# Constant bounds for the experts' places, and counts taken at attention's end

## The chip, the cores and the metric

The kernel runs on one core of one Trainium2 chip. Its measure is the device time in microseconds (us) of one execution of the program. Three runs before the change took 791.21, 792.16 and 792.94 us; the median is 792.16 us. The inputs are drawn once, from a fixed seed.

## The reference, cut to what matters

The program is three layers behind one another, all in 32-bit floats. `x` has 1536 rows (2 batches of 768) and 512 columns.

```python
scores = scale * q @ k.T - slope * dist          # 8 heads, 64 wide
scores = where(first 8 columns or the last 96, scores, -1e9)
x = softmax(scores) @ v                          # attention

expert_idx = argmax(norm(x) @ norm(emb).T / tau) # 8 experts, one per row
for e in range(8):                               # first mixture
    mask = expert_idx == e
    out[mask] = gate_w[mask] * (relu(x[mask] @ w1[e]) @ w2[e])   # 512 -> 1024 -> 512

for e in range(4):                               # second mixture: every row through all four
    out2 += p[:, e] * (relu(out @ v1[e]) @ v2[e])
```

How many rows an expert gets is known only while the program runs. The reference's own routing of its drawn inputs gives the eight experts 171, 247, 155, 177, 135, 215, 231 and 205 rows.

## The kernel before

**Stages.** Attention runs first, over 12 tiles of 128 rows. At its end the rows are scattered to `xs`, a buffer in DRAM with 256 places (`CAP`) for each expert. Then the first mixture goes through the experts one by one, and the second mixture through four experts in two halves each, over chunks of 512 columns.

**The first mixture.** An expert has eight steps (`st`), each with one quarter of its weights: four steps of first products `h` (lines 907 to 909) and four of second products `y` (lines 922 and 923). A number is kept as a high and a low part (`wh`, `wl`; `xh`, `xl`; the two halves of `hhl`), so each weight block takes part in three products for `h`, and in one double-width and one single-width product for `y`. ScalarE writes the high parts, VectorE the low ones. A quarter is split six or seven steps before it is used.

**Arms by rows.** An expert's products need only as many columns as it has rows. Three widths exist, 184, 232 and 256, and TensorE branches on a register (`wide`) that `wider(e)` loads from the table `arm`. `h` has two arms (232, 256), `y` three, once for each of eight half-quarters `f`. Expert 0 has no arms: when its work begins, the counts are not there yet, so both its products run at 256.

**The counts.** In step 1 of expert 0, `offsets()` multiplies `cum` with ones on TensorE (line 793), and from it VectorE makes `cnt` (line 798), `over` and `arm`. GpSimd adds the counts up one by one (line 805) to `off`, the first place of each expert in the list of rows without gaps, and casts it to `offi` (line 806).

**Places.** After expert `e`'s products, a register `o_` is loaded from `offi` (line 943) with the bounds 0 and 1536, and the results go to 256 columns of `x2h` (ScalarE, line 775) and `x2l` (VectorE, line 948) from column `o_` on. What lies behind an expert's own rows is overwritten by the next expert, so the order of the experts is kept. The framework orders readers of `x2h` and `x2l` after all writers whose columns may overlap theirs, by the bounds of `o_`.

**The second mixture** begins with `Unit.hidden` (lines 1039 to 1041): twelve products of 512 columns for each of its blocks, from columns 0 to 511 of `x2h` and `x2l` first. The instructions are written in program order on each engine; the framework adds the waits.

Of the kernel before, what the change touches and what calls it, by code (L numbers as in the profile page):

```python
# [22 lines left out]
P = 128  # L23
# [13 lines left out]
def tile_attention_moe_moe(ctx: ExitStack, tc: tile.TileContext, q, k, v, n_global, n_local,  # L37
# [166 lines left out]
    base = cp.tile([P, T], F32, name="base")  # L204
    rsb = cp.tile([P, T, 8], F32, name="rsb")
    offi = cp.tile([P, NE], I32, name="offi")

    pc = ring.tile([P, 1024], F32, tag="w", name="pc")
    perm = pc[:, 0:2 * CAP].rearrange("p (i n) -> p i n", i=2)
# [82 lines left out]
    def count(t_, pp):  # L292

        while small and small[0][0] <= t_:
            fill()
        nc.tensor.matmul(pp, tri, oh[:, t_, :], start=True, stop=False)
        nc.tensor.matmul(pp, ones, cum[:, t_, :], start=False, stop=True)
        pps[t_] = pp
# [12 lines left out]
                                     xall[:, t_, :], None, bounds_check=NSLOT - 1, oob_is_err=False)  # L311

    xy = []

    def first_rows(xe):
        for i in range(2):
            for c in range(KD):
                nc.tensor.matmul(xy[c][:, i * P:(i + 1) * P], xe[:, i, c * P:(c + 1) * P], ident, start=False, stop=False)  # L320
# [6 lines left out]
    with ExitStack() as at:  # L327
# [387 lines left out]
        rows_x(T - 1, 1)  # L715
        xy.extend([ps_s.tile([P, CAP], F32, tag="s", name="xy") for _ in range(4)])
        add_rows(T - 2)
        count(T - 1, ps_a.tile([P, NE], F32, tag="at", name="pp"))
        fin2(T - 1)
        first_rows(xe)  # L720
        add_rows(T - 1)
        xh0, xl0 = (ring.tile([P, 1024], F32R, tag="w", name="x0").rearrange("p (k n) -> p k n", k=KD) for _ in range(2))
        for c in range(KD):
            nc.scalar.copy(xh0[:, c, :], xy[c])
# [41 lines left out]
    with ExitStack() as mo:  # L766
# [15 lines left out]
        with ExitStack() as m1:  # L782
# [6 lines left out]

            def offsets():  # L790

                pt = ps_t.tile([P, NE], F32, tag="t", name="t")
                nc.tensor.matmul(pt, ones, cum[:, T, :], start=True, stop=True)
                cnt = mp1.tile([P, NE + 1], F32, name="cnt")
                over = mp1.tile([P, NE], F32, name="over")
                arm = mp1.tile([P, NE], I32, name="arm")
                off = mp1.tile([P, NE], F32, name="off")
                nc.vector.tensor_tensor(cnt[:, 0:NE], pt, ebase, ALU.subtract)
                nc.vector.tensor_scalar(over, cnt[:, 0:NE], float(WIDTHS[0]), None, ALU.is_gt)
                nc.vector.scalar_tensor_tensor(arm, cnt[:, 0:NE], float(WIDTHS[1]), over, ALU.is_gt, ALU.add)  # L800
                nc.vector.tensor_reduce(cnt[:, NE:], cnt[:, 0:NE], AX.X, ALU.max)
                nc.vector.scalar_tensor_tensor(flag, cnt[:, NE:], float(CAP) + 0.5, fl[:, 0:1], ALU.is_ge, ALU.max)
                nc.gpsimd.memset(off[:, 0:1], 0.0)
                for e in range(1, NE):
                    nc.gpsimd.tensor_tensor(off[:, e:e + 1], off[:, e - 1:e], cnt[:, e - 1:e], ALU.add)
                nc.gpsimd.tensor_copy(offi, off)
                nc.gpsimd.tensor_tensor(off, off, ebase, ALU.subtract)
                return off, arm

            def offsets2(off):  # L810

# [8 lines left out]
            def records(ri):  # L820
# [2 lines left out]
                    nc.gpsimd.indirect_dma_start(recv[t_], bass.IndirectOffsetOnAxis(ap=ri[:, t_:t_ + 1].bitcast(U32), axis=0),  # L823
                                                 rsrc[:, t_, :], None, bounds_check=NT - 1, oob_is_err=False)
                nc.gpsimd.dma_start(out=rsb, in_=rec.rearrange("(t p) c -> p t c", p=P))

            def wider(e):
                return nc.values_load(sorted_[2][0:1, e:e + 1], engines=(mybir.EngineType.PE,), min_val=0, max_val=2)

            def two_widths(e, wide):  # L830

                if e == 0:
                    yield CAP
                else:
                    with tc.If(wide > 1) as full:
                        yield WIDTHS[2]
                    with full.Else():
                        yield WIDTHS[1]

            def three_widths(e, wide):  # L840

                if e == 0:
                    yield CAP
                else:
                    with tc.If(wide > 0) as over:
                        with tc.If(wide > 1) as full:
                            yield WIDTHS[2]
                        with full.Else():
                            yield WIDTHS[1]
                    with over.Else():  # L850
                        yield WIDTHS[0]

            xr = {}

# [23 lines left out]
            def side(st):  # L878

                if st == 1:  # L880
                    sorted_[0], sorted_[2] = offsets()
                if st == 2:
                    sorted_[1] = offsets2(sorted_[0])
                    nc.gpsimd.memset(x2l.bitcast(F32), 0.0)
                if 2 <= st < 2 + T:
                    square(mp1, st - 2)
                if st == 3 or 2 + T <= st:
                    next(parts, None)
                if st == 8 + T:
                    records(sorted_[1])  # L890
# [1 line left out]
            load_x(1)  # L892
            hp = cycle([ps_h.tile([P, 2, CAP], F32, tag="h", name="h") for _ in range(3)])
            yp = ps_y.tile([P, KD, 2, CAP], F32, name="y")
            wide = None
            for e in range(NE):
                xa, xb = (xh, xl) if e else (xh0, xl0)
                for i in range(4):
                    st = 8 * e + i
                    wh, wl = use(st)  # L900
                    pt = next(hp)
                    for w_ in two_widths(e, wide):
                        for f in range(2):
                            ws = slice(f * P, (f + 1) * P)
                            for c in range(KD):
                                o_, a_, b_ = pt[:, f, 0:w_], xa[:, c, 0:w_], xb[:, c, 0:w_]
                                nc.tensor.matmul(o_, wh[:, c, ws], a_, start=c == 0, stop=False)  # L907
                                nc.tensor.matmul(o_, wh[:, c, ws], b_, start=False, stop=False)  # L908
                                nc.tensor.matmul(o_, wl[:, c, ws], a_, start=False, stop=c == KD - 1)  # L909
                    relu3(pt, hhl[:, 2 * i:2 * i + 2, 0, :], hhl[:, 2 * i:2 * i + 2, 1, :])  # L910
                    split_to(min(st + PRE, W0 + 2))
                    side(st)
                for i in range(4):
                    st = 8 * e + 4 + i
                    wh, wl = use(st)
                    for f in range(2):
                        kf = 2 * i + f
                        for w_ in three_widths(e, wide):
                            a_ = hhl[:, kf, :, 0:w_]
                            for d in range(KD):  # L920
                                ws = slice(d * P, (d + 1) * P)
                                nc.tensor.matmul(yp[:, d, :, 0:w_], wh[:, f, ws], a_, start=kf == 0, stop=False, skip_group_check=True)  # L922
                                nc.tensor.matmul(yp[:, d, 0, 0:w_], wl[:, f, ws], a_[:, 0], start=False, stop=kf == KF - 1, skip_group_check=True)  # L923
# [8 lines left out]
                    if e == NE - 1:  # L932
# [5 lines left out]
                        elif i == 2:  # L938
# [2 lines left out]
                            w_op(0, 3)  # L941
                wide = ahead
                o_ = nc.values_load(offi[0:1, e:e + 1], engines=(mybir.EngineType.Activation, mybir.EngineType.DVE),
                                    min_val=0, max_val=NT)
                for d in range(0, KD, 2):
                    hi, lo = (a[:, d:d + 2, bass.ds(o_, CAP)] for a in (x2h, x2l))
                    split3(yp[:, d:d + 2, 0, :], hi, rest)
# [414 lines left out]
```

## Time and profile before

| | us |
|---|---|
| median of three runs | 792.16 |
| the profiled execution | 791.21 |
| its span, first to last instruction | 789.5 |
| attention's stage | 0 to about 96 |
| first mixture, expert 0 | 95.9 to 119.75 |
| first mixture, to the last `y` product | 119.75 to 269.85 |
| second mixture | 269.85 to the end |

TensorE is busy in 774.6 of the 789.5 us. A group of instructions in the profile has its line, engine, operation, what it writes and reads, its shape, its count, its busy time and mean duration, and the idle time before it. A matmul's duration reaches from its start to its modelled end, and the next one starts before that; how long a series takes is therefore read from the starts, or from a window that holds the series. [...]

### The profile page before, as it was taken

What the parts mean: (1) busy time and instruction counts of PE and PEld (TensorE: products, weight loads), DVE (VectorE), ACT (ScalarE), POOL (GpSimd) and SP (SyncE); (2) the same over time, 40 slices, a digit from 0 to 9 for tenths busy, and PEclk for the clock granted to TensorE, in tenths of its full rate; (3) what the DMA queues carried; (4) which work ended last, traced back from release to release, by engine and by line L of the source; (5) the groups of instructions that cost most, each with busy time, mean ns of one, the idle gap of its engine ahead of it and who ended that gap; (6) DMA issues with size and microseconds to landing.
All of it is one profiled execution on the core that took longest, in us unless ns stands there. A gap on an engine that the chain in (4) does not pass through costs nothing.

```text
span 789.5 us, 14345 instructions
## 1 busy us (share of the span) xinstructions
PE 774.6 (98%) x5450; PEld 706.5 (89%) x5450; DVE 547.1 (69%) x1306; ACT 354.0 (45%) x712; POOL 261.7 (33%) x240
## 2 busy tenths in 40 slices
PE   8999999999999899999999999999999999999996
PEld 5889899999999789999899999999899999989995
DVE  7888676877777446556766766766777766676674
ACT  7899576756655344442232242332233233224221
POOL 2026560160000621451361351352163145136222
PEclk9999999999999999999999999999999999999999
DMA  7996366677765400010000100010001001000111
GB/s 230 319 292 215 127 221 209 213 221 248 238 222 188 154 28 27 28 54 27 28 27 27 54 28 27 27 54 28 27 27 54 28 27 54 1 1 1 54 55 57
DMA packets 32313, 77.97 MB, mean 99 GB/s; under 512 B 3864, under 2 KB 10280, under 8 KB 32224
## 3 DMA queue, kind: packets, MB, share of 16 engines
q1 hardware_dynamic: 29792, 70.36, 27.2%
q0 software_dynamic: 2416, 6.39, 2.2%
q8 instruction: 58, 0.95, 0.5%
q14 instruction: 31, 0.25, 0.1%
q10 hardware_dynamic: 16, 0.02, 0.0%
HBM read 66.22 MB, written 10.53 MB: 97 GB/s over the span
## 4 chain that ended last, share of the span: by engine, by line
PE 84%; DVE 9%; ACT 3%; DMA 1%; issue 1%; POOL 1%; POOLq 0%; ACTq 0%; SPq 0%; DVEq 0%
PE h L1040 10%; PE h L1039 10%; PE h L1041 10%; PE z L1133 9%; PE z L1136 9%; PE z L1135 9%; PE y L922 7%; PE h L907 4%; PE h L909 4%; PE h L908 4%; PE y L923 3%; DVE sh L1090 2%; PE s L501 2%; PE o L542 1%; PE at L528 1%; ACT aa L520 1%
## 5 line engine op out<-in xcount | busy, mean ns | idle before, releaser
L1009 DVE SCALAR_TENSOR_TENSOR xall<-z,rsb,xall 128x256 f32<-128x256 f32 x313 | 135.2, 478 | 35.2 <-PE z L1136 34.6
L1040 PE MATMUL h<-x2l,wh 128*128 128x512 f32 (+1 forms) x400 | 153.5, 384 | 1.2 <-DVE x2l L948 1.2
L1039 PE MATMUL h<-x2h,wh 128*128 128x512 f32 (+1 forms) x400 | 153.5, 384 | 0.9 <-ACT x2h L775 0.9
L1041 PE MATMUL h<-x2h,wl 128*128 128x512 f32 (+1 forms) x400 | 152.7, 382 | 0.0
L1133 PE MATMUL z<-wt,sh 128*128 128x256 f32 x384 | 109.4, 285 | 0.8 <-ACT sh L1098 0.3
L1136 PE MATMUL z<-wt,sl 128*128 128x256 f32 x384 | 108.9, 284 | 0.0
L1135 PE MATMUL z<-wt,sh 128*128 128x256 f32 x384 | 108.6, 283 | 0.0
L1061 POOL TENSOR_TENSOR bl<-h,bh 128x512 fp32r<-128x512 f32 (+1 forms) x25 | 31.9, 1275 | 189.0 <-PE z L1136 164.5
L1076 ACT ACTIVATE ah<-h 128x512 fp32r<-128x512 f32 (+1 forms) x50 | 29.1, 582 | 140.6 <-PE h L1041 140.6
L1040 PEld LDWEIGHTS h<-x2l,wh 128*128 128x128 f32 x400 | 75.8, 189 | 14.9 <-POOL wt L182 1.3
L1039 PEld LDWEIGHTS h<-x2h,wh 128*128 128x128 f32 x400 | 75.7, 189 | 14.6 <-POOL t L175 1.2
L1041 PEld LDWEIGHTS h<-x2h,wl 128*128 128x128 f32 x400 | 75.5, 189 | 14.7
L922 PE MATMUL y<-hhl,wh 128*128 128x464 f32 (+2 forms) x256 | 82.6, 378 | 0.0
L1133 PEld LDWEIGHTS z<-wt,sh 128*128 128x128 f32 x384 | 73.5, 191 | 3.2 <-DVE xall L1009 1.8
L1049 ACT ACTIVATE h<-h 128x512 f32<-128x512 f32 (+1 forms) x50 | 28.7, 573 | 105.1 <-PE h L1041 105.1
L93 DVE TENSOR_TENSOR wl<-raw,wh 128x1024 fp32r<-128x1024 f32 x62 | 75.0, 1230 | 0.0
L1135 PEld LDWEIGHTS z<-wt,sh 128*128 128x128 f32 x384 | 73.6, 192 | 0.8
L1136 PEld LDWEIGHTS z<-wt,sl 128*128 128x128 f32 x384 | 73.5, 192 | 0.3 <-DVE sl L1099 0.3
L182 POOL TENSOR_TENSOR wt<-raw,wt 128x512 fp32r<-128x512 f32 x40 | 51.5, 1297 | 57.7 <-ACT wt L181 50.5
L123 ACT ACTIVATE wh<-raw 128x1024 fp32r<-128x1024 f32 x61 | 64.0, 1057 | 14.2 <-DMA raw<-in_moe_w_dram 12.6
L1055 DVE SCALAR_TENSOR_TENSOR ss<-h,h 128x256 f32<-128x256 f32 (+1 forms) x50 | 20.5, 409 | 69.6 <-ACT h L1049 69.6
L923 PE MATMUL y<-hhl,wl 128*128 128x232 f32 (+2 forms) x256 | 67.8, 265 | 0.0
(210 smaller groups left out, 1894.1 us busy)
## 6 DMA issues: line engine op xcount, KB each, us to landing
raw<-in_moe_w_dram SPq DMA_DIRECT2D x96, 512.0 KB, 3.9
xs<-zt SPq DMA_DIRECT2D x4, 1024.0 KB, 7.3
xr<-xs SPq DMA_DIRECT2D x14, 256.0 KB, 4.7
v<-in_v_dram SPq DMA_DIRECT2D x12, 256.0 KB, 5.4
k<-in_k_dram SPq DMA_DIRECT2D x11, 256.0 KB, 5.2
q<-in_q_dram SPq DMA_DIRECT2D x11, 256.0 KB, 5.0
vwin<-in_v_dram SPq DMA_DIRECT2D x10, 192.0 KB, 5.6
xe<-xs SPq DMA_DIRECT2D x2, 256.0 KB, 2.8
```

What stands on the lines that cost most here:

```text
L93: eng.tensor_tensor(lo, r, hi.bitcast(F32), ALU.subtract)
L123: nc.scalar.activation(hi, r, AF.Copy)
L182: nc.gpsimd.tensor_tensor(t[:, 1], src, t[:, 0].bitcast(F32), ALU.subtract)
L922: nc.tensor.matmul(yp[:, d, :, 0:w_], wh[:, f, ws], a_, start=kf == 0, stop=False, skip_group_check=True)
L923: nc.tensor.matmul(yp[:, d, 0, 0:w_], wl[:, f, ws], a_[:, 0], start=False, stop=kf == KF - 1, skip_group_check=True)
L1009: nc.vector.scalar_tensor_tensor(a_, src[:, i], w_, a_, ALU.mult, ALU.add)
L1039: nc.tensor.matmul(pt, wh[:, d, ws], x2h[:, d, cs], start=d == 0, stop=False)
L1040: nc.tensor.matmul(pt, wh[:, d, ws], x2l[:, d, cs], start=False, stop=False)
L1041: nc.tensor.matmul(pt, wl[:, d, ws], x2h[:, d, cs], start=False, stop=d == KD - 1)
L1133: nc.tensor.matmul(pt[:, i], hh[:, f, ts_], wh[:, f, :], start=(o_ < 3 or pt is not prods[o_][3]) and i == f == 0, stop=False, skip_group_ ...
L1135: nc.tensor.matmul(pt[:, i], hh[:, f, ts_], wl[:, f, :], start=False, stop=False, skip_group_check=True)
L1136: nc.tensor.matmul(pt[:, i], hl[:, f, ts_], wh[:, f, :], start=False, stop=f == 1, skip_group_check=True)
```

## The change

Two things are changed.

First, the counts are summed at attention's end. The tile `pp` of the last count gets a second half, which two small products fill with the sums of all rows; `sizes()` makes `cnt`, `over` and `arm` from it on VectorE, and the register for expert 0 is loaded there (`ahead = wider(0)`). So expert 0's `y` goes through three arms like the others'; its `h` stays at 256. Because a narrow arm leaves columns of `yp` unwritten, VectorE sets columns 184 to 255 to zero in step 1.

Second, the place `o_` of expert `e` gets the bounds max(0, 1536 - 256 (8 - e)) and min(1536, 256 e), which hold whenever no expert has over 256 rows. For expert 0 both are 0, so its place is a constant on VectorE. So that the table keeps within the bounds in every case, `offi` is now the larger of `off` and a table `least`, taken by VectorE, instead of a cast by GpSimd.

```diff
+    def sizes(pt):
+        nc.vector.tensor_tensor(cnt[:, 0:NE], pt, ebase, ALU.subtract)
+        nc.vector.tensor_scalar(over, cnt[:, 0:NE], float(WIDTHS[0]), None, ALU.is_gt)
+        nc.vector.scalar_tensor_tensor(arm, cnt[:, 0:NE], float(WIDTHS[1]), over, ALU.is_gt, ALU.add)
+    def wider(e):
+        return nc.values_load(arm[0:1, e:e + 1], engines=(mybir.EngineType.PE,), min_val=0, max_val=2)
...
-        count(T - 1, ps_a.tile([P, NE], F32, tag="at", name="pp"))
+        pp = ps_a.tile([P, 2, NE], F32, tag="at", name="pp")
+        count(T - 1, pp[:, 0])
+        nc.tensor.matmul(pp[:, 1], ones, cum[:, T - 1, :], start=True, stop=False)
+        nc.tensor.matmul(pp[:, 1], ones, oh[:, T - 1, :], start=False, stop=True)
         fin2(T - 1)
+        sizes(pp[:, 1])
         first_rows(xe)
         add_rows(T - 1)
+        ahead = wider(0)
...
-                pt = ps_t.tile([P, NE], F32, tag="t", name="t")
-                nc.tensor.matmul(pt, ones, cum[:, T, :], start=True, stop=True)
...
-                nc.vector.tensor_tensor(cnt[:, 0:NE], pt, ebase, ALU.subtract)
-                nc.vector.tensor_scalar(over, cnt[:, 0:NE], float(WIDTHS[0]), None, ALU.is_gt)
-                nc.vector.scalar_tensor_tensor(arm, cnt[:, 0:NE], float(WIDTHS[1]), over, ALU.is_gt, ALU.add)
...
-                nc.gpsimd.tensor_copy(offi, off)
+                least = mp1.tile([P, NE], I32, name="least")
+                nc.gpsimd.iota(least, [[CAP, NE]], base=NT - NE * CAP, channel_multiplier=0)
+                leastf = mp1.tile([P, NE], F32, name="leastf")
+                nc.gpsimd.tensor_copy(leastf, least)
+                nc.vector.tensor_tensor(offi, leastf, off, ALU.max)
...
-            wide = None
+            wide = ahead
...
-                    for w_ in two_widths(e, wide):
+                    for w_ in two_widths(wide) if e else (CAP,):
...
+                    if st == 1:
+                        nc.vector.memset(yp[:, :, :, WIDTHS[0]:], 0.0)
...
-                        for w_ in three_widths(e, wide):
+                        for w_ in three_widths(wide):
...
-                                    min_val=0, max_val=NT)
+                                    min_val=max(0, NT - (NE - e) * CAP), max_val=min(NT, e * CAP))
```

In the lists that follow, a row is a line of the kernel, an instruction with what it writes and reads, its shape, and the engines or queues whose semaphores it waits for (the number there is the same in all).

TensorE, where the last expert's `y` ends and the second mixture begins (`h<-x2h`, `h<-x2l`). Before:

```order
L922 MATMUL y<-hhl,wh 128x2x184
L923 MATMUL y<-hhl,wl 128x184
L845 UNCONDITIONAL_BRANCH
L1039 MATMUL h<-x2h,wh 128x512 [waits Activation_49,Pool_49]
L1040 MATMUL h<-x2l,wh 128x512 [waits DVE_49,Pool_49]
L1041 MATMUL h<-x2h,wl 128x512
```

With the change:

```order
L928 MATMUL y<-hhl,wh 128x2x184
L929 MATMUL y<-hhl,wl 128x184
L336 UNCONDITIONAL_BRANCH
L1045 MATMUL h<-x2h,wh 128x512 [waits PE_49,Pool_49]
L1046 MATMUL h<-x2l,wh 128x512 [waits Pool_49]
L1047 MATMUL h<-x2h,wl 128x512 [waits DVE_49]
```

The first product no longer waits for ScalarE and the second no longer for VectorE; the third, whose weights' low part VectorE writes, now has that wait itself.

TensorE, where expert 0's `h` ends and its `y` begins. Before:

```order
L908 MATMUL h<-x_1686,wh 128x256
L909 MATMUL h<-x_1685,wl 128x256
L922 MATMUL y<-hhl,wh 128x512 [waits Activation_49]
L923 MATMUL y<-hhl,wl 128x256 [waits DVE_49]
L922 MATMUL y<-hhl,wh 128x512
```

With the change (the widest arm's first row and the way to it):

```order
L912 MATMUL h<-x_1704,wh 128x256
L913 MATMUL h<-x_1703,wl 128x256
L336 COMPARE_AND_BRANCH
L337 COMPARE_AND_BRANCH
L928 MATMUL y<-hhl,wh 128x512 [waits DVE_49,PE_49,Activation_49]
L929 MATMUL y<-hhl,wl 128x256
```

Two branches stand ahead of the first `y` product, and that product waits for VectorE.

VectorE, step 1 of expert 0 (`wl` is a quarter's low part, `hhl` the low part of `h`). Before:

```order
L93 TENSOR_TENSOR wl<-raw,wh 128x1024 [waits DMAHW0_49,Pool_49]
L93 TENSOR_TENSOR wl<-raw,wh 128x1024 [waits DMAHW0_49]
L798 TENSOR_TENSOR cnt<-t,ebase 128x8 [waits DVE_49,PE_49]
L799 TENSOR_SCALAR over<-cnt 128x8 [waits DVE_49]
L800 SCALAR_TENSOR_TENSOR arm<-cnt,over 128x8 [waits DVE_49]
L801 TENSOR_REDUCE cnt<-cnt 128x1
L802 SCALAR_TENSOR_TENSOR flag<-cnt,fl 128x1 [waits DVE_49]
L780 SCALAR_TENSOR_TENSOR hhl<-h,hhl 128x2x256 [waits Activation_49]
L93 TENSOR_TENSOR wl<-raw,wh 128x1024 [waits DMAHW7_49,Pool_49]
```

With the change:

```order
L93 TENSOR_TENSOR wl<-raw,wh 128x1024 [waits DMAHW0_49,Pool_49]
L93 TENSOR_TENSOR wl<-raw,wh 128x1024 [waits DMAHW0_49]
L827 TENSOR_REDUCE cnt<-cnt 128x1
L828 SCALAR_TENSOR_TENSOR flag<-cnt,fl 128x1 [waits DVE_49]
L836 TENSOR_TENSOR offi<-leastf,off 128x8 [waits Pool_49]
L918 MEMSET y 128x8x72
L814 SCALAR_TENSOR_TENSOR hhl<-h,hhl 128x2x256 [waits Activation_49]
L93 TENSOR_TENSOR wl<-raw,wh 128x1024 [waits DMAHW7_49]
```

Three operations have gone from here to attention's end, and two have come: `offi`, which waits for GpSimd, and the memset of `y`.

## Rows read from the trace of the kernel before

**Rows 1.** The page's busy time, share of the span and instructions of each engine.

```profile
PE 774.6 (98%) x5450; PEld 706.5 (89%) x5450; DVE 547.1 (69%) x1306; ACT 354.0 (45%) x712; POOL 261.7 (33%) x240
```

**Rows 2.** What TensorE waited for: us in total, times, longest us.

```profile
PE h L1040 <- DVE x2l L948: 1.2, 2, 1.0
...
PE h L1039 <- ACT x2h L775: 0.9, 1, 0.9
```

**Rows 3.** TensorE's second products by shape: count | busy us, mean ns | idle.

```profile
L922 PE MATMUL y<-hhl,wh 128*128 128x368 f32 x96 | 27.8, 361 | 0.0
...
L922 PE MATMUL y<-hhl,wh 128*128 128x512 f32 x64 | 23.0, 398 | 0.0
```

**Rows 4.** Windows: us, busy us (count) per engine, clock, DMA share, GB/s; second products.

```profile
107.67:119.75 12.08, 12.08 (x75) 10.71 (x74) 8.72 (x12) 10.36 (x21) 7.54 (x8) 1.00 0.67 228
131.27:143.37 12.10, 12.10 (x74) 10.71 (x73) 8.20 (x11) 9.69 (x16) 0.00 (x0) 1.00 0.54 184
154.09:163.85 9.76, 9.76 (x75) 9.76 (x73) 8.47 (x10) 5.70 (x7) 7.93 (x6) 1.00 0.73 226
215.60:226.84 11.24, 11.24 (x74) 10.48 (x73) 7.77 (x9) 6.66 (x8) 0.00 (x0) 1.00 0.70 223
```

**Rows 5.** TensorE timeline, one product after the experts' end [idle, releaser].

```profile
269.74 0.27 PE L923 MATMUL y<-hhl,wl 128*128 128x232 f32 x1
270.92 0.47 PE L1039 MATMUL h<-x2h,wh 128*128 128x512 f32 x1 [0.91 <-ACT x2h L775]
272.37 0.47 PE L1040 MATMUL h<-x2l,wh 128*128 128x512 f32 x1 [0.98 <-DVE x2l L948]
...
274.40 0.79 PE L1040 MATMUL h<-x2l,wh 128*128 128x512 f32 x1 [0.18 <-DVE x2l L948]
...
277.31 0.40 PE L1041 MATMUL h<-x2h,wl 128*128 128x512 f32 x1
```

**Rows 6.** The window in which the clock is lower, columns as in Rows 4.

```profile
273.60:277.00 3.40, 3.22 (x8) 2.12 (x7) 0.71 (x2) 0.01 (x1) 1.18 (x1) 0.50 0.22 89
```

**Rows 7.** TensorE timeline, first and last of twelve undisturbed first-layer products.

```profile
293.50 0.40 PE L1039 MATMUL h<-x2h,wh 128*128 128x512 f32 x1
...
296.02 0.39 PE L1041 MATMUL h<-x2h,wl 128*128 128x512 f32 x1
```

**Rows 8.** VectorE timeline: the last expert's last write.

```profile
273.65 0.69 DVE L948 TENSOR_TENSOR x2l<-y,rest 128x512 f32 x1
```

**Rows 9.** TensorE timeline around the count's product.

```profile
101.67 0.28 PE L909 MATMUL h<-x,wl 128*128 128x256 f32 x1
101.79 0.18 PE L793 MATMUL t<-cum,ones 128*128 128x8 bf16 x1
...
102.03 0.28 PE L908 MATMUL h<-x,wh 128*128 128x256 f32 x1
```

**Rows 10.** TensorE's sequencer: branches and register load, ns min/median/max, first and last start.

```profile
L846 PEldq COMPARE_BRANCH  x64: 65/179/417, 129.5 to 267.0; - x64
...
L835 PEldq COMPARE_BRANCH  x32: 65/208/1378, 116.6 to 254.8; - x32
...
L828 PEldq TENSOR_LOAD <-arm x7: 302/311/487, 114.6 to 243.6; - x7
```

**Rows 11.** GpSimd timeline, the running sums of counts.

```profile
105.80 2.85 POOL L805 TENSOR_TENSOR off<-off,cnt 128x1 f32<-128x1 f32 x7 [3.20 <-DVE cnt L798]
108.71 0.20 POOL L806 CAST offi<-off 128x8 int32<-128x8 f32 x1
```

**Rows 12.** VectorE timeline, second first-product stage of expert 0.

```profile
103.23 2.35 DVE L93 TENSOR_TENSOR wl<-raw,wh 128x1024 fp32r<-128x1024 f32 x2
...
110.50 1.22 DVE L93 TENSOR_TENSOR wl<-raw,wh 128x1024 fp32r<-128x1024 f32 x1
```

**Rows 13.** VectorE's nearest operations to the new memset.

```profile
L530 DVE COPY ats<-at 128x512 f32<-128x512 f32 x10 | 6.9, 687 | 2.0 <-PE at L528 2.0
...
L386 DVE MEMSET zt<- 128x512 f32 x1 | 0.5, 485 | 0.1
```

More of the change, by code (lines that the diff above doesn't have):

```diff
@@ L206, in tile_attention_moe_moe @@
     offi = cp.tile([P, NE], I32, name="offi")
+    cnt = cp.tile([P, NE + 1], F32, name="cnt")
+    over = cp.tile([P, NE], F32, name="over")
+    arm = cp.tile([P, NE], I32, name="arm")
     pc = ring.tile([P, 1024], F32, tag="w", name="pc")
@@ L311, in scatter, with two_widths, three_widths @@
                                      xall[:, t_, :], None, bounds_check=NSLOT - 1, oob_is_err=False)
+    def sizes(pt):
[4 more added lines that the diff above has]
+        return nc.values_load(arm[0:1, e:e + 1], engines=(mybir.EngineType.PE,), min_val=0, max_val=2)
+    def two_widths(wide):
+        with tc.If(wide > 1) as full:
+            yield WIDTHS[2]
+        with full.Else():
+            yield WIDTHS[1]
+    def three_widths(wide):
+        with tc.If(wide > 0) as upper:
+            with tc.If(wide > 1) as full:
+                yield WIDTHS[2]
+            with full.Else():
+                yield WIDTHS[1]
+        with upper.Else():
+            yield WIDTHS[0]
     xy = []
@@ L790, in offsets @@
             def offsets():
-                pt = ps_t.tile([P, NE], F32, tag="t", name="t")
-                nc.tensor.matmul(pt, ones, cum[:, T, :], start=True, stop=True)
-                cnt = mp1.tile([P, NE + 1], F32, name="cnt")
-                over = mp1.tile([P, NE], F32, name="over")
-                arm = mp1.tile([P, NE], I32, name="arm")
                 off = mp1.tile([P, NE], F32, name="off")
-                nc.vector.tensor_tensor(cnt[:, 0:NE], pt, ebase, ALU.subtract)
-                nc.vector.tensor_scalar(over, cnt[:, 0:NE], float(WIDTHS[0]), None, ALU.is_gt)
-                nc.vector.scalar_tensor_tensor(arm, cnt[:, 0:NE], float(WIDTHS[1]), over, ALU.is_gt, ALU.add)
                 nc.vector.tensor_reduce(cnt[:, NE:], cnt[:, 0:NE], AX.X, ALU.max)
@@ L805, in offsets @@
                     nc.gpsimd.tensor_tensor(off[:, e:e + 1], off[:, e - 1:e], cnt[:, e - 1:e], ALU.add)
-                nc.gpsimd.tensor_copy(offi, off)
+                least = mp1.tile([P, NE], I32, name="least")
[3 more added lines that the diff above has]
+                nc.vector.tensor_tensor(offi, leastf, off, ALU.max)
                 nc.gpsimd.tensor_tensor(off, off, ebase, ALU.subtract)
-                return off, arm
+                return off
             def offsets2(off):
@@ L825, in records @@
                 nc.gpsimd.dma_start(out=rsb, in_=rec.rearrange("(t p) c -> p t c", p=P))
[L827 to L851, printed above, removed]
             xr = {}
@@ L880, in side @@
                 if st == 1:
-                    sorted_[0], sorted_[2] = offsets()
+                    sorted_[0] = offsets()
                 if st == 2:
```

## The prediction

> **What bounds the kernel now.** I began with the page's first part: TensorE is busy for 774.6 of the 789.5 us [rows 1], so time is won only by giving TensorE less to do or by taking away one of its few waits. Next come its waits. Two of them touch the change: the second mixture's first products wait 0.9 us for ScalarE's `x2h` and 1.2 us for VectorE's `x2l` [rows 2]. The list of products by shape then shows the arms at work: 96 `y` products of 368 columns and 64 of 512 [rows 3]. An expert has 32 double-width `y` products (8 half-quarters by 4), so two experts run at 256, and three at 184. By the reference's routing the three are experts 2, 3 and 4 (155, 177 and 135 rows), and the two at 256 are expert 1 (247 rows), whose count needs it, and expert 0, which has 171 rows and runs at 256 only because it has no arms. So with arms expert 0 takes the narrowest. Last I read windows over whole `y` stages, and the timeline where the experts end.
>
> **Term A: expert 0's `y` at 184.** Its stage now takes 12.08 us. Expert 2's, at 184 with its arms, takes 9.76 us with as many products and the same two transposes inside, and with TensorE busy in all of it [rows 4]. That is 12.08 - 9.76 = 2.32 us less, branches paid: the row of expert 2 has them in it. What the branches cost by themselves is read from expert 1, at 256 with arms: 12.10 us against 12.08 without [rows 4], so 0.02 us for eight passes. The sequencer's own rows give a branch a median of 179 ns [rows 10], so nearly all of that lies beside products that are already issued. Bounds for the branches: 0.02 us, and 8 x 0.179 = 1.4 us if nothing covered them; I take the first, inside expert 2's row. [...]
>
> **Term B: the count's product goes.** It stands between two `h` products whose starts are 102.03 - 101.79 = 0.24 us apart with it, where a neighbour takes 0.12 us [rows 9]: 0.12 us less.
>
> **Term C: the wait at the experts' end.** The last `y` product, 232 columns, starts at 269.74 us. The next starts only at 270.92, the one behind it after another 0.98 us idle, the eighth after 0.18 us more, and the fifteenth starts at 277.31 us [rows 5]. Undisturbed, twelve products of 512 columns start from 293.50 to 296.02 us, a step of 2.52 / 11 = 0.229 us [rows 7]. A product of 232 columns would at that rate be over after 0.229 x 232 / 512 = 0.10 us, so the series could start at 269.84, and its fifteenth at 269.84 + 14 x 0.229 = 273.05 us. The delay is 277.31 - 273.05 = 4.26 us. Only 2.07 us of it is the three idle pieces. [...]
>
> With the new bounds the last four experts start at columns 512, 768, 1024 and 1280 at the lowest, so none of them can reach columns 0 to 511; the first block of the second mixture depends on experts 0 to 3 alone, which are long done. The lists of the change show the waits gone from the first two products. The third waits for VectorE's low part of its weights, which was written before the last expert ended. So I take the whole 4.26 us, and if there is no gap, no lower clock. What is late next: ScalarE and VectorE still write the last expert's results, until 273.65 + 0.69 = 274.34 us [rows 8], while TensorE runs its first three blocks until 269.84 + 36 x 0.229 = 278.1 us in the same count of time. Only the fourth block needs a buffer of `h` back from VectorE, whose operation on the first block follows that last write. Some 3 us stay; the wait doesn't come back there. Bounds: 2.07 us (idle pieces alone, clock still lower) and 4.26 us.
>
> **What is added, and what hides it.** The two products of the sums stand ahead of products that wait for `xe`, and VectorE's three `sizes` operations move there from step 1, into a stretch where it waits for ScalarE's copies: nothing. The register load costs the sequencer 311 ns, 487 at most [rows 10]. It is queued behind eight wide `xy` products, and what is queued behind it is expert 0's first `h` product, which waits for ScalarE's and VectorE's split of `xy` anyway; in the loop a load stands between two steps and the products by it are idle for 0.0 us [rows 3]. I take 0, with 0.5 us as the other end. ScalarE and VectorE get some eight plain branches each; if these cost as much as TensorE's 179 ns, that is 1.4 us of lag off TensorE's path.
>
> In step 1 VectorE now takes `offi` and sets `yp` to zero. `offi` waits for GpSimd. There the running sums took 2.85 us from 105.80 us on, after a wait of 3.20 us for `cnt`, and the cast 0.20 us [rows 11]. With `cnt` made earlier they start at 102.60 and end at 105.45; an iota and a cast at 0.2 to 0.28 us each bring this to about 106.0. VectorE's two low parts end at 103.23 + 2.35 = 105.58 us [rows 12], two tiny operations follow, so it waits for GpSimd 0.1 us or so. The memset has 576 elements a partition: an SBUF memset of 512 took 485 ns, a copy out of PSUM 687 ns [rows 13]; I take 0.7 us, so it ends near 106.9 us. TensorE wants to begin `y` at 107.67 - 0.12 = 107.55 us: 0.6 us to spare. Behind the memset, VectorE's queue holds the low part of the third `h` block, wanted some 5 us later, and the low part of step 8's weights, written at 110.50 to 111.72 us now [rows 12] and wanted at 119.75 - 2.44 = 117.3 us. Cost 0; without cover, 0.5 us. ScalarE is busy for 10.36 us in expert 0's `y` stage [rows 4] and will lag by 0.6 to 2 us into the next `h` stage; what it writes there, and `yp`, are wanted only by the `y` stage some 11 us on.
>
> **Sum.** 2.32 + 0.12 + 4.26 = 6.70 us. The profiled execution took 791.21 us (span 789.5, 1.71 around it), so it would take 784.5 us. It was the fastest of the three runs; the median lies 0.95 us higher, and I can put that to no row. The forecast is for the median: 792.16 - 6.70 = 785.5 us.
>
> **Rivals.**
> 1. The clock falls at the second mixture's start even without idle TensorE. Then the 3.40 - 1.83 = 1.57 us of [rows 6] are paid still: 787.0 us. For it: I see the fall once, so its cause is inferred. Against: it follows right on the two gaps. 7 in 100.
> 2. The wait stays: some other reader or writer of the last expert's results holds the first block, as the four writes of ScalarE and VectorE are where they were. Then only A and B remain, 2.44 us: 789.7 us. Against it stands the list of waits. 6 in 100.
> 3. Branches and the load are exposed in expert 0, whose first `y` product waits for a memset 0.6 us ahead, so that the sequencer has less of a lead than at the others: up to 1.4 + 0.5 us, 787.4 us. 5 in 100.
> 4. Expert 0 takes another arm: at 232 the stage is 11.24 us [rows 4], a gain of 0.84 instead of 2.32 us, 786.9 us; at 256 it is 787.8 us. The shapes agree with the counts, so 3 in 100.
> 5. Slower. [...] 3 in 100. [...]
> 6. Something not seen eats most of the gain: about 791 us. 2 in 100.
>
> **How the numbers follow.** The forecast itself has the remaining 74 in 100. The range starts a little under the profiled execution's 784.5, at 783.8, and reaches to 788.0, which takes in rivals 1, 3 and 4 and the other ends of the small costs (branches 1.4, load 0.5, memset 0.5 us); outside are rivals 2, 5, 6 and some scatter. What a measurement here can tell from no change is about 0.2%, 1.6 us. Faster by more: the forecast and rivals 1 to 4, less a little, 0.94; within it 0.03; slower 0.03.
>
> **What would show it.** In the changed kernel's profile: 128 `y` products of 368 columns and 32 of 512; expert 0's `y` stage 9.8 us; no wait of TensorE for `x2h` or `x2l` at the experts' end, the first `h` product there 0.1 us behind the start of the last `y`, and the clock at 1.00 throughout; the second mixture as long as before from its fifteenth product on. A wait of TensorE for the memset at expert 0's `y`, a new gap before the fourth block, or a gap after a branch would show a term wrong.

## The result and the profile after

The changed kernel took 785.18 us (median of 784.92, 785.10, 785.27 and 786.71), the kernel before, beside it, 791.68 us (791.10 to 792.94). The ratio is 0.9911, with a 95% interval of 0.9893 to 0.9929: 6.5 us less. In a later series of runs it was 785.78 against 792.52 us, ratio 0.9912 (0.9897 to 0.9926). The profiled execution took 784.92 us, with a span of 783.2.

The page's busy line, against [rows 1]: TensorE does 3.7 us less and is still the bound.

```profile
PE 770.9 (98%) x5451; PEld 705.1 (90%) x5451; DVE 548.6 (70%) x1308; ACT 354.0 (45%) x712; POOL 262.9 (34%) x241
```

TensorE's waits, longest in sum first (us in total, times, longest). Neither `x2h` nor `x2l` is among them any more, as they were in [rows 2]; what is left at the top was there before.

```profile
PE pt L578 <- DVE zb L414: 1.3, 1, 1.3
PE lp L246 <- DVE xall L276: 1.0, 2, 0.8
PE xy L349 <- DMA xe<-xs: 0.5, 1, 0.5
```

The second products by shape, against [rows 3]: 32 products went from 512 to 368 columns, with no idle time ahead of either kind.

```profile
L928 PE MATMUL y<-hhl,wh 128*128 128x368 f32 x128 | 37.2, 361 | 0.0
...
L928 PE MATMUL y<-hhl,wh 128*128 128x512 f32 x32 | 11.5, 399 | 0.0
```

Windows over expert 0's `h` and `y` stages (columns as in [rows 4]; the `h` stage took 11.80 us before, from its first product at 95.87 to 107.67 us):

```profile
95.92:107.61 11.69, 11.69 (x99) 11.66 (x97) 7.10 (x13) 7.00 (x11) 10.79 (x14) 1.00 0.66 206
107.61:117.44 9.83, 9.83 (x74) 9.83 (x73) 8.92 (x13) 8.08 (x16) 5.78 (x3) 1.00 0.72 243
```

TensorE's timeline from the last `y` product to the fifteenth product of the second mixture, and the window of that series. It took 269.74 to 277.31 us, 7.57 us, in [rows 5]; now 267.48 to 270.79, 3.31 us, without an idle piece and with the clock, given in a window as the share of TensorE's full clock that was granted, at 1.00 where [rows 6] had 0.50.

```profile
267.48 0.27 PE L929 MATMUL y<-hhl,wl 128*128 128x232 f32 x1
267.58 0.40 PE L1045 MATMUL h<-x2h,wh 128*128 128x512 f32 x1
267.82 0.39 PE L1046 MATMUL h<-x2l,wh 128*128 128x512 f32 x1
...
270.79 0.39 PE L1047 MATMUL h<-x2h,wl 128*128 128x512 f32 x1
```

```profile
267.58:270.79 3.21, 3.21 (x16) 2.64 (x15) 1.38 (x2) 1.67 (x5) 3.21 (x3) 1.00 0.10 15
```

VectorE in step 1 of expert 0 and GpSimd's sums beside it, against [rows 11, 12]. The memset ends at 107.46 us; the first `y` product starts at 107.61.

```profile
103.29 2.38 DVE L93 TENSOR_TENSOR wl<-raw,wh 128x1024 fp32r<-128x1024 f32 x2
105.59 0.15 DVE L827 TENSOR_REDUCE cnt<-cnt 128x1 f32<-128x8 f32 x1
105.78 0.16 DVE L828 SCALAR_TENSOR_TENSOR flag<-cnt,fl 128x1 int32<-128x1 f32 x1
106.63 0.17 DVE L836 TENSOR_TENSOR offi<-leastf,off 128x8 int32<-128x8 f32 x1 [0.70 <-POOL leastf L835]
106.92 0.54 DVE L918 MEMSET y<- 128x576 f32 x1
```

```profile
102.73 3.53 POOL L831 TENSOR_TENSOR off<-off,cnt 128x1 f32<-128x1 f32 x7
106.21 0.13 POOL L833 IOTA least<- 128x8 int32 x1
106.41 0.19 POOL L835 CAST leastf<-least 128x8 f32<-128x8 int32 x1
```

From expert 0's first product to TensorE's last instruction the profile before has 686.30 us, the one after 679.74: 6.56 less. The start (95.87 and 95.92) and the tail behind TensorE's last instruction (7.33 and 7.54 us) lie outside.

### The profile page after: what moved, and what is told of

Same layout as the page of the kernel before. It is cut to its first block, busy times and chain, and to the rows that moved or that the text cites. A ratio compares the mean times of both kernels' runs of the same rounds, so it can differ in the third digit from the quotient of the medians.

```text
span 783.2 us, 14345 instructions
## 1 busy us (share of the span) xinstructions
PE 770.9 (98%) x5451; PEld 705.1 (90%) x5451; DVE 548.6 (70%) x1308; ACT 354.0 (45%) x712; POOL 262.9 (34%) x241
## 4 chain that ended last, share of the span: by engine, by line
PE 84%; DVE 9%; ACT 3%; issue 1%; DMA 1%; POOL 1%; POOLq 0%; SPq 0%; DVEq 0%; ACTq 0%
PE h L1045 10%; PE h L1046 10%; PE h L1047 10%; PE z L1139 9%; PE z L1142 9%; PE z L1141 9%; PE y L928 7%; PE h L911 4%; PE h L912 4%; PE h L913 4%; PE y L929 3%; DVE sh L1096 2%; PE s L530 2%; PE at L557 1%; PE o L571 1%; ACT aa L549 1%
## 5 line engine op out<-in xcount | busy, mean ns | idle before, releaser
L928 PE MATMUL y<-hhl,wh 128*128 128x368 f32 (+2 forms) x256 | 80.5, 374 | 0.0
L929 PE MATMUL y<-hhl,wl 128*128 128x184 f32 (+2 forms) x256 | 66.7, 261 | 0.0
```

## Experiments

"The series" below is the time from the start of the last `y` product to the start of the fifteenth product of the second mixture: 7.57 us before, 3.31 after. Single times of one kernel differ by 1 to 8 us, so the stages in the profiles carry more than the medians do.

### The two parts, each alone

bounds_only is the kernel before with the bounds and the `least` table; arms_only is the changed kernel with the old bounds.

```diff
bounds_only, against before:
-                nc.gpsimd.tensor_copy(offi, off)
...
+                nc.vector.tensor_tensor(offi, leastf, off, ALU.max)
-                                    min_val=0, max_val=NT)
+                                    min_val=max(0, NT - (NE - e) * CAP), max_val=min(NT, e * CAP))
arms_only, against after:
-                                    min_val=max(0, NT - (NE - e) * CAP), max_val=min(NT, e * CAP))
+                                    min_val=0, max_val=NT)
```

> The kernel before with only the constant bounds on the experts' places (and the clamped table of places that they need); expert 0 has no arms and the counts stay in step 1. Theory (three separate terms, all on TensorE): only the wait at the experts' end goes, 4.26 us, so about 791.7 - 4.3 = 787.4 us, expert 0's second products still 12.1 us long, and no window of lower clock at 270 us. Rival (the bounds gain only the idle pieces, the clock falls all the same): 2.1 to 2.7 us, about 789.3 us.

> The changed kernel with the old bounds 0 and 1536 on the experts' places; arms for expert 0 and the counts at attention's end stay. Theory: 2.25 us at expert 0's second products and 0.11 us at its first ones, so about 791.7 - 2.4 = 789.3 us, with the two waits of TensorE for x2h and x2l back at the experts' end and the lower clock behind them. Rival (the terms lean on each other, for example the shorter expert 0 is paid back by late weights once the rest is as before): under 1 us, about 791 us.

bounds_only took 789.57 us (ratio to before 0.9966, 0.9952 to 0.998; before 792.48 there), arms_only 790.27 (0.9974, 0.9964 to 0.9984). The TensorE timelines of both at the experts' end, bounds_only first:

```profile
271.54 0.27 PE L927 MATMUL y<-hhl,wl 128*128 128x232 f32 x1
271.64 0.40 PE L1043 MATMUL h<-x2h,wh 128*128 128x512 f32 x1
...
274.85 0.39 PE L1045 MATMUL h<-x2h,wl 128*128 128x512 f32 x1
```

```profile
268.71 0.27 PE L929 MATMUL y<-hhl,wl 128*128 128x232 f32 x1
...
270.05 0.47 PE L1045 MATMUL h<-x2h,wh 128*128 128x512 f32 x1 [1.07 <-ACT x2h L809]
271.51 0.47 PE L1046 MATMUL h<-x2l,wh 128*128 128x512 f32 x1 [0.98 <-DVE x2l L954]
...
276.34 0.39 PE L1047 MATMUL h<-x2h,wl 128*128 128x512 f32 x1
```

The bounds alone bring the series to 3.31 us, all of term C; without them the waits are back and it takes 7.63. Expert 0's stages, read in the same way, do the reverse: `y` 12.07 us in bounds_only, 9.81 in arms_only. So the two parts are separate, each in its own stage. The medians show less: 2.9 and 2.2 us, 5.1 in sum, where the whole change gave 6.5; by its median alone bounds_only would lie nearer to its rival's 789.3 us. In their profiles pieces elsewhere fill the difference. Expert 3's `h` stage took 11.77 and 11.78 us instead of 10.74 (told of below); in bounds_only the experts also began 0.82 us later and the tail was 8.36 us, in arms_only 0.28 later and 7.04. With these the profiled 791.21 us of the kernel before lead to 789.83 and 789.92; the two executions took 789.80 and 789.96. Whether the same is there in every run was not seen.

### The clock behind the waits

gap_filled is the kernel before with eleven products into a free buffer ahead of the second mixture, so that TensorE works where it waited. act_wide and dve_wide are the changed kernel with the old bounds for one engine's writes only; each engine loads its own place for that, VectorE a second one (`od`) that keeps the other bounds.

```diff
gap_filled, against before:
+                if e == NE - 1:
+                    fp = ps_t.tile([P, 2, CAP], F32, tag="t", name="t")
+                    for _ in range(11):
+                        nc.tensor.matmul(fp, hhl[:, 0, 0, 0:P], hhl[:, 0], start=True, stop=True)
act_wide, against after (dve_wide: the other way round):
+                oa = nc.values_load(offi[0:1, e:e + 1], engines=(mybir.EngineType.Activation,),
+                                    min_val=0, max_val=NT)
...
-                    hi, lo = (a[:, d:d + 2, bass.ds(o_, CAP)] for a in (x2h, x2l))
...
+                    hi, lo = x2h[:, d:d + 2, bass.ds(oa, CAP)], x2l[:, d:d + 2, bass.ds(od, CAP)]
...
```

> The kernel before, with eleven products of 512 columns into an unused buffer put on TensorE between the last expert's last product and the second mixture's first one. The waits for x2h and x2l stay, but TensorE works through them (11 x 0.229 = 2.5 us). Theory (the clock fell because TensorE idled): the clock stays at 1.00, the fifteenth product of the second mixture is 2.5 to 2.9 us late instead of 4.26, so about 791.7 - 1.5 = 790.2 us. Rival (the clock falls at this place whatever TensorE does): the lower clock is still there behind the filling products, and the time is 791.7 us or a little more.

> The changed kernel with one of its two sets of bounds given back: ScalarE's copies into x2h have bounds 0 to 1536 again, VectorE's writes of x2l keep the narrow ones. So TensorE's products that read x2h wait for ScalarE's last copy again, those that read x2l do not wait. Theory (the gain at the experts' end is two waits, and the halved clock is what the idle time between them brought): the first product waits about 1.0 us, the clock stays at 1.00 since one short wait is all that is idle, and the fifteenth product starts 3.31 + 1.2 to 1.7 us after the last y product (changed kernel 3.31, kernel before 7.57): 786.4 to 786.9 us. Rival (any wait at this place brings the halved clock): the series is late by some 1.5 us more, 6.1 us or over from the last y product to the fifteenth, 787.9 to 788.5 us. The times of single runs differ by 1 to 2 us, so the stage decides.

> The other half: VectorE's writes of x2l have bounds 0 to 1536, ScalarE's copies into x2h the narrow ones. The product that reads x2l (the second, and the eighth of the next part) waits for VectorE's last subtraction, which comes after ScalarE's copy, so the wait is the later of the two. Theory (the clock fell because of the idle time): idle about 2 us in sum, and from the last y product to the fifteenth product either 3.31 + 2.0 to 2.9 us with the clock at 1.00, or, as long an idle time as in the kernel before, 7.57 us again with 0.50: 787.5 to 789.4 us. Rival (the first wait, for ScalarE, is the one that costs and VectorE's is hidden behind it): under 3.31 + 1.0 us and 786 us.

Each kernel's TensorE timeline, with a window behind its waits; gap_filled:

```profile
273.38 0.40 PE L1043 MATMUL h<-x2h,wh 128*128 128x512 f32 x1
...
275.58 0.50 PE L1044 MATMUL h<-x2l,wh 128*128 128x512 f32 x1 [0.40 <-DVE x2l L952]
...
277.30 0.39 PE L1045 MATMUL h<-x2h,wl 128*128 128x512 f32 x1
```

```profile
270.82:277.30 6.48, 6.08 (x27) 4.54 (x26) 2.77 (x4) 2.46 (x6) 4.62 (x4) 1.00 0.25 82
```

act_wide, whose last `y` product starts at 273.32 us:

```profile
274.66 0.47 PE L1050 MATMUL h<-x2h,wh 128*128 128x512 f32 x1 [1.07 <-ACT x2h L957]
...
276.69 0.50 PE L1050 MATMUL h<-x2h,wh 128*128 128x512 f32 x1 [0.42 <-ACT x2h L957]
...
278.64 0.39 PE L1052 MATMUL h<-x2h,wl 128*128 128x512 f32 x1
```

```profile
274.66:278.64 3.98, 3.56 (x15) 2.63 (x16) 2.65 (x4) 1.32 (x3) 3.32 (x3) 1.00 0.36 132
```

dve_wide, whose last `y` product starts at 271.57 us:

```profile
274.81 0.47 PE L1051 MATMUL h<-x2l,wh 128*128 128x512 f32 x1 [2.73 <-DVE x2l L959]
...
279.45 0.40 PE L1052 MATMUL h<-x2h,wl 128*128 128x512 f32 x1
```

```profile
275.22:278.63 3.41, 3.41 (x10) 2.59 (x9) 1.38 (x2) 0.64 (x2) 1.43 (x2) 0.50 0.45 143
```

The same place in the program, by how long TensorE was idle there:

| kernel | idle pieces, us | clock granted behind them | series, us |
|---|---|---|---|
| after | none | 1.00 | 3.31 |
| gap_filled | 0.40 | 1.00 | 6.59, 2.56 of it the added products |
| act_wide | 1.07, 0.42 | 1.00 | 5.32 |
| before | 0.91, 0.98, 0.18 | 0.50 | 7.57 |
| dve_wide | 2.73 | 0.50 | 7.88 |

The clock stays at 1.00 where TensorE has work, although all else there is as before (gap_filled), and where it is idle for 1.49 us in two pieces; it was lower behind 2.07 and 2.73 us. So the lower clock came of the idle time and not of the place: the forecast's view, and rival 1 falls. The same comes at two other places below, behind a wait in memset4 and in expert 3's `h` stage. The sum of the pieces alone doesn't tell when: in that stage dve_wide has the lower clock behind four pieces of 1.46 us in sum. dve_wide's own rival falls too; of the two outcomes that its theory left open it has the second, with 7.88 us where 7.57 was expected. In act_wide the series was 0.3 us over the expected range although the clock stayed: the idle column counts from a product's modelled end. The first product starts 1.34 us behind the last `y` product instead of 0.10, so a wait shown as 1.07 cost 1.24; the second, shown as 0.42, delayed the seventh product from a step of 0.23 to one of 0.81 us (275.88 to 276.69), 0.58.

By time gap_filled is no gain: 792.69 us, ratio 1.0005 (0.9996 to 1.0014), where 790.2 was expected. Its series is only 0.98 us shorter than before, since the added products run for 2.56 us and one wait is left: the fifteenth product is 3.28 us late, where 2.5 to 2.9 was expected. Not even the 0.98 shows in the median. In the profile, expert 3's `h` stage took 0.48 us more, the experts began 0.49 us later and the tail was 8.93 us against 7.33; from 791.21 us that leads to 792.80, and this execution took 792.86. Whether the others lost it in the same places was not seen. act_wide and dve_wide were run once, at 792.69 and 793.72 us, above what was expected: expert 3's `h` stage took 15.47 and 14.88 us in those runs instead of 10.74 (told of below). They are read by the stage alone.

### The memset's cover

memset4 does the memset of `yp` four times. h232 gives expert 0's `h` its arms as well (232 and 256 columns), so that the `y` products are wanted earlier; it also narrows the `relu3` of expert 0 to 232 columns and zeroes the rest of `hhl` ahead of the experts, which the cut below leaves out. h232_early is h232 with the memset of `yp` ahead of the experts.

```diff
memset4:
-                        nc.vector.memset(yp[:, :, :, WIDTHS[0]:], 0.0)
+                        for _ in range(4):
+                            nc.vector.memset(yp[:, :, :, WIDTHS[0]:], 0.0)
h232:
-                    for w_ in two_widths(wide) if e else (CAP,):
+                    for w_ in two_widths(wide):
...
h232_early, besides:
+            nc.vector.memset(yp[:, :, :, WIDTHS[0]:], 0.0)
...
-                    if st == 1:
-                        nc.vector.memset(yp[:, :, :, WIDTHS[0]:], 0.0)
```

> The changed kernel with the zeroing of yp's tail done four times over, three more VectorE instructions of some 0.45 to 0.54 us each between the offsets and the first expert's second products. Theory (the trace after shows the zeroing end 0.15 us before the first of these products starts): TensorE waits there for VectorE 1.2 to 1.5 us, and that stage begins so much later. Rival (the prediction's own 0.6 us of cover): it waits 0.75 to 1.05 us.

> The changed kernel with arms for expert 0's first products too (232 or 256 columns), on the register that is now loaded before them; expert 0's rows above 232, of which these inputs have none, are left out. Theory (the register load and a branch at the start of expert 0 cost TensorE nothing, and its first products take what those of experts with 232 columns take, 10.7 us instead of 11.7): 0.9 to 1.0 us less, about 784.2 us, with the gain seen in the window of expert 0's first products. Rival (load and branch are in the open there): 0.5 us or more of it is lost to a gap before the first product, 784.8 us or above.

> As h232 (expert 0's first products too go through arms of 184 and 232 columns; the rows above 232 of expert 0 are left out), but the zeroing of yp stands ahead of the experts' loop, where VectorE is idle, and not in the first expert's second step. Theory (what h232 lacked was the wait of 0.73 us for that zeroing, behind POOL's sums): no wait between expert 0's last first product and its first second product, that stage 11.1 us instead of 11.7 and nothing given back, 0.6 to 0.9 us less than the changed kernel, 784.3 to 784.6 us. Rival (the register load and the branches ahead of the first of the products are exposed now, since the count is known only some 3 us before): the stage begins later by 0.3 to 1 us, and the time is that of the changed kernel, 785 to 785.6 us.

memset4, VectorE, then TensorE's first `y` product, then a window behind it:

```profile
107.31 0.17 DVE L836 TENSOR_TENSOR offi<-leastf,off 128x8 int32<-128x8 f32 x1 [0.98 <-POOL leastf L835]
107.59 0.54 DVE L919 MEMSET y<- 128x576 f32 x1
108.33 0.54 DVE L919 MEMSET y<- 128x576 f32 x1 [0.20 <-DVE y L919]
...
109.80 0.54 DVE L919 MEMSET y<- 128x576 f32 x1 [0.20 <-DVE y L919]
```

```profile
110.48 0.41 PE L929 MATMUL y<-hhl,wh 128*128 128x368 f32 x1 [2.28 <-DVE y L919]
```

```profile
110.90:114.30 3.40, 3.40 (x15) 3.40 (x15) 3.33 (x7) 0.00 (x0) 3.15 (x3) 0.50 0.31 93
```

TensorE waited 2.28 us, more than both expectations: each further memset cost 0.73 us, not 0.45 to 0.54, since it waits 0.20 us for the one before it. It also shows the cover to be thinner than 0.15 us: with expert 0's first `h` product at 96.36 us and the `h` stage's 11.69 us, `y` was wanted at 108.05, and the first memset alone ended at 108.13. Nor were the 0.15 us of the profile after to spare. The products here and in h232, which did wait for the memset, start 0.14 and 0.15 us behind its end, so the product in the profile after, 0.15 behind, came as early as the memset let it. GpSimd's seven sums took 3.75 us here, 3.53 in the profile after. The same holds for two later profiles of the changed program (records_spread and records_late, whose TensorE and VectorE work is that of after): the `h` stage took 11.93 and 11.92 us there, 0.24 us more. And here, at another place, the clock was granted at 0.50 behind 2.28 us of idle time; the `y` stage took 11.41 us instead of 9.83.

h232 in its first `y` product, and h232_early over its `h` stage:

```profile
109.02 0.41 PE L930 MATMUL y<-hhl,wh 128*128 128x368 f32 x1 [0.73 <-DVE y L920]
```

```profile
97.03:108.01 10.98, 10.98 (x98) 10.95 (x97) 7.21 (x13) 5.92 (x9) 10.26 (x12) 1.00 0.64 212
```

In h232 the narrower `h` is met by a wait of 0.73 us for that memset: the stage took 11.87 us, no gain over 11.69. With the memset ahead of the experts, the wait is gone and the stage takes 10.98 us (11.1 was expected), 0.71 us less. The times don't show it: h232 787.17 us (0.9927, 0.9913 to 0.994), h232_early 786.40 against 793.13 (0.9914, 0.9897 to 0.993), the changed kernel 0.9911 and 0.9912. No version beat the changed kernel by more than its runs differ.

### What differs from run to run

Eight of the first ten profiles have TensorE idle by 0.3 to 2.7 us in sum at 167 to 175 us, with no wait that would explain it. GpSimd's twelve indirect DMAs for the records begin at 152 to 157 us and end at 171 to 176. records_spread gives them out one a step; records_late puts a GpSimd copy of a later tile ahead of them.

```diff
records_spread:
...
+                    yield
...
-                    records(sorted_[1])
+                    sorted_[2] = records(sorted_[1])
+                if 8 + T <= st:
+                    next(sorted_[2], None)
records_late:
-                if st == 8 + T:
+                if st == 24 + T:
+                    nc.gpsimd.tensor_copy(mp1.tile([P, 1], F32, name="late"), hhl[:, 0, 0, 0:1].bitcast(F32))
                     records(sorted_[1])
```

> The changed kernel with the twelve indirect DMAs of the records issued one in each of the steps 20 to 31 instead of one after the other in step 20. Theory (the runs differ by 1 to 3 us because TensorE's instructions come late while this burst of DMAs runs, seen as idle time that no wait explains at 160 to 176 us, 0.3 to 0.9 us in most profiles and some 3 us in one): that idle time goes, the runs lie closer together, and the median is 0.3 to 1 us below the changed kernel's, 784.2 to 784.9 us. Rival (the idle time there has another cause, or comes wherever DMAs run): it is still there or moves, and the median is within 0.3 us of the changed kernel's or above it, since the last records come later.

> The changed kernel with the burst of the records' twelve indirect DMAs really put off: GpSimd first copies one column of expert 4's first hidden tile, so the burst, which runs from 152 to 172 us in every profile so far (in records_spread too, where GpSimd had nothing to wait for), starts at about 187 us and ends at about 207. Theory (TensorE's idle time that no wait explains, 0.2 to 2.7 us at 167 to 175 us in eight of ten profiles, comes with the last part of that burst): none at 167 to 175, and some, if any, at 200 to 210 us; the time is that of the changed kernel, 785.2 us, within 1 us. Rival (it comes from the place in the program, the narrow arms of expert 3): still idle at 167 to 175 us. Second rival (it has neither place nor burst and comes by chance): idle time somewhere else or none.

> The changed kernel itself once more, beside the two others on one chip, for the size of the gain and of what differs from run to run: 785.2 us as the median, within 1 us, runs from 784.9 to some 788 us, 6 to 8 us below the kernel before. By stages: expert 0's second products 9.83 us, 3.31 us from the last product of the experts to the fifteenth of the second mixture, clock 1.00 there; what differs from the first profile lies in the start of the experts, in idle time at 160 to 176 us and behind the last product.

records_spread did not do what it says: GpSimd has nothing else to wait for, so its DMAs still ran one behind the other from 153.27 us on. It is one more run of the changed program: 786.78 us (784.96 to 791.28). records_late, GpSimd's timeline and TensorE's:

```profile
188.94 1.02 POOL L853 DMA_INDIRECT rec<-rsrc,ri  x1 [0.62 <-POOL late L894]
...
204.67 1.97 POOL L853 DMA_INDIRECT rec<-rsrc,ri  x1 [0.30 <-issue]
```

```profile
205.36 0.27 PE L913 MATMUL h<-xl,wh 128*128 128x232 f32 x1 [0.83 <-issue]
206.09 0.27 PE L914 MATMUL h<-xh,wl 128*128 128x232 f32 x1 [0.47 <-issue]
```

The burst moved by some 36 us and the idle time with it: none at 167 to 175, 1.4 us at 204 to 207. So in this one profile it went with the end of that burst and not with expert 3's arms. One piece doesn't fit: records_spread has 0.27 us at 192.55, some 21 us behind its burst. Whether such a burst makes TensorE's instructions come late, and why four profiles show nothing, was not tried. The time is no better: 786.84 us (784.90 to 789.28). after_again had no such idle time, its series took 3.31 us, and its runs lie at 785.28 to 786.24.

This idle time costs far more than its column says. Windows over expert 3's whole `h` stage, after and h232, and then over the stretch in which the clock was lower, in h232, act_wide, dve_wide and h232_early:

```profile
161.58:172.32 10.74, 10.74 (x98) 10.74 (x97) 7.13 (x10) 6.09 (x9) 8.88 (x7) 1.00 0.71 237
163.00:179.01 16.01, 13.27 (x98) 12.82 (x97) 8.88 (x11) 6.64 (x9) 7.30 (x8) 0.89 0.58 176
172.70:176.10 3.40, 3.40 (x19) 3.40 (x18) 2.96 (x4) 2.79 (x4) 1.11 (x1) 0.50 0.32 25
173.59:176.98 3.39, 3.39 (x18) 3.39 (x18) 2.81 (x4) 2.92 (x4) 1.11 (x1) 0.50 0.16 10
172.83:176.23 3.40, 3.40 (x19) 3.40 (x18) 3.20 (x4) 2.55 (x4) 1.11 (x1) 0.50 0.25 16
170.79:177.60 6.81, 6.41 (x29) 6.08 (x29) 4.78 (x6) 4.52 (x6) 1.11 (x1) 0.50 0.47 102
```

| profile | idle pieces in the stage, sum, us | clock of 0.50 in it | expert 3's `h` stage, us |
|---|---|---|---|
| before, after, memset4 | none | no | 10.74 |
| gap_filled | 0.31 | no | 11.22 |
| arms_only, records_spread, bounds_only | 0.53, 0.64, 0.86 | no | 11.78, 11.80, 11.77 |
| dve_wide | 1.46 | yes | 14.88 |
| h232_early | 2.07 | yes | 17.24 |
| act_wide | 2.21 | yes | 15.47 |
| h232 | 2.64 | yes | 16.01 |

The clock fell here too behind idle pieces, and the stage took 4.1 to 6.5 us more. after_again's took 11.01 us without a piece in the column. With expert 0's stages, the start of the experts, the series and the tail, this stage accounts to 0.1 us for the profiled runs of act_wide, dve_wide, h232 and h232_early, which lie 6.5 to 8.8 us above the profiled 784.92 of the change. The profiled runs of h232 and h232_early are the slowest of their six; how much of this the other runs have was not seen.

## Why the prediction was right

**Term A, 2.32 us: 2.25.** The `y` stage went from 12.08 to 9.83 us; it was forecast from expert 2's 9.76. Its eight passes with branches can therefore cost at most 0.07 us more there than at expert 2, and rivals 3 to 5 fall with it: expert 0 took the narrowest arm, and no `y` product of the shapes shown stood behind an idle engine.

**Term B, 0.12 us: 0.11**, from 11.80 to 11.69 us. The prediction read the row wrongly: the product at 101.79 us is the count's own, and the two `h` products around it start at 101.67 and 101.83. Up to the `h` product at 102.03 it is 0.36 us where two steps take 0.24, so the 0.12 stands.

**Term C, 4.26 us: 4.26**, from 7.57 to 3.31 us, by the bounds alone (bounds_only, arms_only). Rival 1 is ruled out by gap_filled and act_wide, rival 2 by the list of waits, and no new gap came ahead of the fourth block. The three idle pieces, 2.07 us in sum, cost more than that: they delayed their products by 1.08, 1.22 and 0.57 us, 2.87 in sum, by starts in [rows 5] less the undisturbed steps. The other 1.4 came with the lower clock, granted at 0.50 behind them, where it was 1.00 in the `y` windows of [rows 4], in which TensorE is never idle. Its 8 products took 3.40 us [rows 6], and 8 undisturbed steps of 0.229 us are the 1.83 of rival 1; the 1.57 us between the two takes in the eighth product's step too.

**What hid the additions** was mis-sized in one step, the one that gave the memset 0.6 us to spare. It had nothing to spare in the profile after and came 0.24 us late in others. GpSimd's sums were taken at the 2.85 us of [rows 11], but moved up they run beside two of VectorE's `wl` operations instead of one, and took 3.52 to 3.76. VectorE waited 0.70 us for them where 0.1 was forecast. The memset itself took 0.54 us, not 0.7. It cost nothing or a quarter of a microsecond; that the forecast's 0 came out in the first profile was luck.

**Sum.** 2.25 + 0.11 + 4.26 = 6.62 us by stages, 6.56 by TensorE's first and last instruction, 6.5 and 6.7 us by the medians. The 0.95 us between the profiled run before and the median, which the prediction could put to no row, fits what differs from profile to profile of all these kernels: the start of the experts (95.66 to 97.15 us), expert 3's `h` stage with its idle time and lower clock (10.74 to 17.24) and the tail (7.04 to 8.93). From the fifteenth product to TensorE's last instruction the first ten profiles agree to 0.09 us (504.83 to 504.92).

## What to carry to other kernels

Where a write's place is known only at run time, give it the tightest bounds that hold: the dependence tracker orders readers by them, and here two numbers took away a wait that the data never needed. Price a wait of the bounding engine by the starts of the series behind it, not by its idle column: 2.07 us of idle time cost 4.26, by late steps and by the lower clock behind it, and in expert 3's `h` stage of h232 2.64 us cost 5.27. When work is moved earlier, ask beside what it will now run, and take its duration from there: GpSimd's sums, moved beside a second `wl` operation, took 3.53 us instead of 2.85.

## What the runs showed of the hardware that was not expected

One of GpSimd's adds on 128x1 elements takes 0.19 us by itself, and 1.04 where it starts inside one of VectorE's 1024-element `wl` operations. In the profile after:

```profile
103.54 1.04 POOL L831 TENSOR_TENSOR off<-off,cnt 128x1 f32<-128x1 f32 x1
```

```profile
103.29 1.24 DVE L93 TENSOR_TENSOR wl<-raw,wh 128x1024 fp32r<-128x1024 f32 x1
```

The kernel before has one such add, of 1.23 us, in a sum of 2.85; the changed one has a second, of 1.06, in its sum of 3.53. Put the long ones at 0.19 and both sums come to 1.81 us, so the whole difference is the second long add. The profile of bounds_only shows the adds without it: there all seven start behind the second `wl` operation, none runs beside one, and the sum took just that:

```profile
106.63 1.81 POOL L805 TENSOR_TENSOR off<-off,cnt 128x1 f32<-128x1 f32 x7 [3.20 <-DVE cnt L798]
```

The add of 1.04 us ends at 104.58 us, 0.05 behind the `wl` operation in which it starts (103.29 + 1.24 = 104.53); the other two long adds end 0.05 us behind theirs as well. Why an add lasts so long there, no row shows.
